# A decode block on one core: TensorE's share of the scores cut to 8 positions in every other middle step, the maximum taken behind the next products, 24 heads of W_o in two loads

## The chip, the cores and the metric

One core of a Trainium2 chip runs the whole program. The metric is device time in microseconds (us) of one execution; the time before is the median of 3 runs. Engines: TensorE (PE, with its weight loads PEld), VectorE (DVE), ScalarE (ACT), GpSimd (POOL), and SyncE (SP), which issues nearly all transfers.

## The reference

A decode step of a transformer block for a batch of 2 with one query each: layer norm, attention over a cache of 8192 positions with 32 heads of 128, output projection and residual, then a second layer norm and a gated feed-forward part with ReLU.

```python
def _A_ref(x, k_cache, v_cache, wq, wo):      # x [2,1,512], caches [2,32,8192,128]
    q = (x @ wq).reshape(B, Sq, Hq, Dh) ...
    scores = einsum("bhqd,bhkd->bhqk", q, k) * (Dh ** -0.5)
    p = softmax(scores)
    o = einsum("bhqk,bhkd->bhqd", p, v)
    return o.reshape(B, Sq, Hq * Dh) @ wo
h  = x + _A_ref(layernorm(x), ...)
h2 = h + _B_ref(layernorm(h), W_gate, W_up, W_down)   # F = 1376; down(relu(gate) * up)
```

Each cache is 134 MB in bf16, and every byte of both is needed once.

## The kernel before

**Steps.** The two batches by 16 pairs of heads make N = 32 steps; L = 31 is the last. Step i holds one pair: partitions 0 to 63 have the first head, 64 to 127 the second, and each partition has NT = 128 positions of 128 numbers, 32 KB, for K and as much for V. kbuf and vbuf have two such buffers each, used in turn. A step's K is one transfer of 4 MB and so is its V (in two or four pieces for the last three).

**Scores.** The positions of a step are shared by share(i). VectorE takes the first nv: products(i) (L335) multiplies K by the query in place, scores(i) halves the width from 128 to 8 by four additions (L350) and sums the rest (L354) into scol; then pm (L358) is the maximum of each partition. TensorE takes the last npe, in scores_pe(i): chunks of 8 positions are transposed (L309), copied to SBUF by ScalarE (L311) and multiplied by the query (L300); ScalarE copies the row (L316), TensorE turns it back (L319), and ScalarE puts it into scol (L325). npe is 24 in step 0, 16 in steps 1 to 28, 32 in steps 29 and 30, and 8 in step 31.

**Softmax.** largest(i) brings pm of all partitions together by a matmul into the PSUM tile mx_ps (L365); exponentials(i) takes the minimum nm of the negated values on VectorE (L377), and ScalarE computes the exponentials into pgz (L380) and their sums into zc.

**Values.** values(i, part) multiplies half of V by pgz in 16 matmuls (L396); after part 1 ScalarE copies the result into pv (L402). A group is four steps (the last one is cut into 2, 1 and 1). At its end diagonals picks the outputs out of pv (L411), sums adds zc over the partitions into z_ps, shares takes the reciprocal rz, and normalise writes the heads' columns ocol. Steps 30 and 31 use values_cols instead (L423), a matmul for every position.

**Output projection.** SETS lists the sets of heads of W_o, each with its first head, number of heads, partitions and place in wbig. A set has its rows spread over the partitions, so that few long runs are moved; spread(k) (VectorE) and the first lines of attend_set(k) bring ocol into the same order (or_ps), and the rest multiplies. The sets are heads 0 to 15; 16 (on 16 partitions, with a further copy, placed); 17; 18 and 19; 20 to 23; 24 to 27. Heads 28 to 31 are a load of their own. Sets are used as soon as their last group is normalised, in batch 1.

**Buffers.** mx_ps, z_ps, or_ps and the layer norm's small tiles share one PSUM buffer, the tag mx, which has one copy: each must be read before the next is written.

**Order.** The order on each engine is the program's (manual_schedule): engines run their own instructions in order and wait for one another by semaphores. SyncE's queue is in order too. The loop over steps is:

```python
for i in range(L):
    sums(i - 2); scores_pe(i); products(i)
    shares(i - 2); normalise(i - 2); attend_set(...)   # where i - 2 ends a group
    values(i - 1, 0); scores(i); largest(i); exponentials(i)
    load K(i + 2); values(i - 1, 1); diagonals(i - 1); load V(i + 1)
```

K(i+2) goes into the buffer that scores(i) has just done with, V(i+1) into that of values(i-1). Steps L-1 and L are written out behind the loop, with the loads of W_gate, W_up (into kbuf's first buffer) and W_down between, then the second layer norm and the feed-forward part (hn, g_ps L576, u_ps, d_ps L606).

Of the kernel before, what the change touches and what calls it, by code (L numbers as in the profile page):

```python
# [13 lines left out]
def _free(t, offset, dims):  # L14

    return bass.AP(tensor=t.tensor, offset=t.offset + offset, ap=[t.ap[0]] + [list(d) for d in dims])


def _dram(t, offset, dims):
    return bass.AP(tensor=t.tensor, offset=t.offset + offset, ap=[list(d) for d in dims])  # L20
# [3 lines left out]
def kernel(  # L24
# [24 lines left out]
    ROW = NT * Dh  # L49
    NG = Hq // 2  # L50
    NPE = NT // 4
    NPE_MID = NT // 8
    NPE_LAST = NT // 16
    TPC = 8
    VG = 4
    EPS = 1e-5
# [9 lines left out]

    SETS = [(0, 16, P, 0), (16, 1, 16, 16), (17, 1, P, 24), (18, 2, P, 25), (20, 4, P, 27), (24, 4, P, 32)]
    WO_T = 36  # L70
    HM = Hq - 4

    assert Sq == 1 and Hkv == Hq and Dh == P and D == KC * P and Hq == 32 and NPE % TPC == NPE_MID % TPC == NPE_LAST % TPC == 0
    assert F == 11 * P - AGAIN

    big = ctx.enter_context(tc.tile_pool(name="big", bufs=1))
# [28 lines left out]
    ocol = consts.tile([P, Hq, B], bf16)  # L105
    hm = consts.tile([P, FC, B], bf16)

    SROWS = [n * Dh // w for _, n, w, _ in SETS]
    sizes = [r for r in sorted(set(SROWS)) if r > 1]
    quot = {r: consts.tile([P, Dh // r], bf16, name=f"quot{r}") for r in sizes}  # L110
    rest = {r: consts.tile([P, r], bf16, name=f"rest{r}") for r in sizes}
    orow = [consts.tile([P, r, B], bf16, name=f"orow{k}") for k, r in enumerate(SROWS)]
    placed = consts.tile([P, B, 16], bf16)
    sel = consts.tile([B, B, HALF], bf16)

    QZ = 2 * NPE // 4
# [7 lines left out]
    N = len(steps)  # L124

    def wo_set(k):
        return wbig[:, SETS[k][3] * D:]

    def load_kv(cache, buf, i, pieces=1, which=None):
        b, g = steps[i]  # L130
# [25 lines left out]
    with tc.manual_schedule():  # L156
# [77 lines left out]
        nc.vector.tensor_copy(qz[:, :, :, QZ - 2:QZ], qT_ps.rearrange("p (g j) b -> p b g j", j=2))  # L234


        for k, ((h0, n, w, _), r) in enumerate(zip(SETS, SROWS)):
            nc.sync.dma_start(
                out=wo_set(k)[0:w, 0:r * D],
                in_=_dram(A_wo, h0 * Dh * D, ([[r * D, P]] if w == P else [[r * D, 4], [4 * r * D, 4]]) + [[1, r * D]]),  # L240
            )
        nc.sync.dma_start(
            out=wbig[:, WO_T * D:(WO_T + Hq - HM) * D].rearrange("p (h n) -> p h n", n=D),
            in_=_dram(A_wo, HM * Dh * D, [[D, P], [Dh * D, Hq - HM], [1, D]]),
# [35 lines left out]

        def share(i):

            npe = NPE_LAST if i == L else NPE if i >= L - 2 else NPE_MID if i else NPE - TPC
            return NT - npe, npe

        def scores_pe(i):


            b, g = steps[i]
            kt = kbuf[:, i % 2, :]  # L290
            nv, npe = share(i)
            U = npe // 4
            row_ps = ps.tile([2 * U, 4 * P], f32, tag="row")
            kTs = {}

            def times_q(c0):
                for k in range(0, TPC, 4):
                    u = (c0 + k) // 4
                    z0 = QZ - 2 - 2 * u
                    nc.tensor.matmul(  # L300
                        out=row_ps, lhsT=qz[:, b, g, z0:z0 + 2 * U],
                        rhs=kTs[c0][:, k * P:(k + 4) * P], start=(u == 0), stop=(u == U - 1),
                    )
# [12 lines left out]
            nc.scalar.activation(out=rows, in_=row_ps, func=ACT.Copy)  # L316
            sc_ps = ps.tile([P, 4, U, 2], f32, tag="row", name="sc_ps")
            for t in range(4):
                nc.tensor.transpose(  # L319
                    sc_ps[:, t].rearrange("p u j -> p (u j)"), rows[:, t * P:(t + 1) * P], ident_f[0:2 * U, 0:2 * U],  # L320
                )
            scols[i] = small.tile([P, NT], f32, tag="scol", name="scol")
            for j in range(2):
                r = slice(j * HALF, (j + 1) * HALF)
                nc.scalar.activation(  # L325
                    out=scols[i][r, nv:NT].rearrange("p (u t) -> p t u", t=4), in_=sc_ps[r, :, :, j], func=ACT.Copy,
                )

        def products(i):

            b, g = steps[i]
            kt = kbuf[:, i % 2, :]
            nv, _ = share(i)
            kv = _free(kt, 0, [[Dh, nv], [1, Dh]])
            nc.vector.tensor_tensor(  # L335
                out=kv, in0=kv, in1=_free(qrep, (b * NG + g) * Dh, [[0, nv], [1, Dh]]), op=ALU.mult,
            )
# [91 lines left out]

        def spread(k):  # L430

            h0, n, w, _ = SETS[k]
            if SROWS[k] == 1:
                return None
            nq = Dh // SROWS[k]
            sps = []
            for b in range(B):
                sp = small.tile([P, P], bf16, tag="spread", name="sp", bufs=4)
                nc.vector.tensor_tensor(
                    out=_free(sp, 0, [[nq, n], [1, nq]]), in0=_free(ocol, h0 * B + b, [[B, n], [0, nq]]),  # L440
                    in1=_free(quot[SROWS[k]], 0, [[0, n], [1, nq]]), op=ALU.mult,
                )
                if w != P:
                    nc.vector.tensor_copy(
                        _free(placed, b * 16, [[1, 4], [4, 4]]), _free(sp, 0, [[4, 4], [1, 4]]),
                    )
                    sp = placed[:, b, :]
                sps.append(sp)
            return sps

        def attend_set(k, sps):

            h0, _, w, _ = SETS[k]
            r = SROWS[k]
            rows = ocol[:, h0:h0 + 1, :]
            if sps is not None:
                or_ps = ps.tile([P, B, r], f32, tag="mx")
                for b in range(B):
                    nc.tensor.matmul(out=or_ps[0:w, b, :], lhsT=sps[b], rhs=rest[r], start=True, stop=True)
                rows = orow[k]  # L460
                nc.scalar.activation(out=rows[0:w], in_=or_ps[0:w].rearrange("p b c -> p c b"), func=ACT.Copy)
            for c0 in range(r):
                for c in range(KC):
                    nc.tensor.matmul(
                        out=att_ps[:, c, :],
                        lhsT=wo_set(k)[0:w, c0 * D + c * P:c0 * D + (c + 1) * P], rhs=rows[0:w, c0, :],
                        start=(k == 0 and c0 == 0 and c == 0), stop=False, skip_group_check=True,
                    )

# [8 lines left out]
        def spreads(i):  # L478

            if i not in groups or groups[i][0] < B - 1:  # L480
                return
            _, g0, n = groups[i]
            for k, (h0, m, _, _) in enumerate(SETS):
                if 2 * g0 < h0 + m <= 2 * (g0 + n):
                    yield k, spread(k)

        for i in range(L):
            if i >= 2:
                sums(i - 2)
            scores_pe(i)  # L490
            products(i)
            if i - 2 in groups:
                shares(i - 2)
                normalise(i - 2)
            for k, sps in spreads(i - 2):
                attend_set(k, sps)
            if i >= 1:
                values(i - 1, 0)
            scores(i)
            largest(i)  # L500
            exponentials(i)
            if i + 2 < N:
                load_kv(A_k_cache, kbuf, i + 2)
            if i == L - 2:
                load_kv(A_v_cache, vbuf, i, 2, [1])
            if 1 <= i < L - 1:
                values(i - 1, 1)
                diagonals(i - 1)
            if i + 1 < L:

                load_kv(A_v_cache, vbuf, i + 1, 1 if i < L - 3 else 2, [0] if i == L - 3 else None)
            if i == NG // 2:
                nc.sync.dma_start(out=wd_sb[:, FC - 1, :], in_=_dram(B_W_down, FSETS[-1][0] * D, [[D, P], [1, D]]))


        scores_pe(L)
        products(L)
        values(L - 2, 1)
        load_kv(A_v_cache, vbuf, L, pieces=4)
        for w, src, n in ((0, B_W_gate, KC), (1, B_W_up, KC // 2)):  # L520
            for c in range(0, KC, n):
                nc.sync.dma_start(  # L522
                    out=wgu[:, w, c:c + n], in_=_dram(src, c * P * F, [[F, P], [P * F, n], [1, F]]),
                )
# [123 lines left out]
```

## Time and profile before

| | |
|---|---|
| time, median of 3 runs | 662.05 us (661.96 to 662.15) |
| profiled execution | 661.76 us, span 660.0 us |
| granted TensorE clock, mean | 0.818 |
| busy: VectorE, TensorE, ScalarE | 551.9, 432.5, 154.7 us |
| moved | 281.48 MB, mean 426 GB/s |
| chain that ended last | DMA 52%, VectorE 42%, TensorE 4% |
| VectorE's idle time before products, for K | 40.1 us over 32 steps |
| VectorE's idle time before nm, for mx_ps | 23.8 us over 32 steps |

The span is the time from the first to the last instruction of the one execution that was profiled; its own time has some 1.8 us around that. In the profile's page, L335 is line 335 of the kernel. Busy digits are tenths of each of 40 equal slices of the span. In the timeline a line gives the start, the length, the engine, the source line and operation, what is written and read with the shapes, how many instructions are merged into it, and in brackets the idle time before them with what ended it. In the groups, what follows the bar is total busy time and the mean of one in ns. In the stretches of time, busy time and number of instructions of PE, PEld, DVE, ACT and POOL are followed by the granted TensorE clock, the share of DMA time and GB/s.

### The profile page before, as it was taken

The page shows a single profiled execution, that of the slowest core. Times are in us where ns is not written, and L with a number is a line of the kernel's source. Part 1 is how long each engine was busy: PE and PEld are TensorE (multiplying, and loading weights), DVE is VectorE, ACT ScalarE, POOL GpSimd, SP SyncE. Part 2 cuts the span into 40 slices and gives each one's busy share as a digit, 9 for nine tenths or more (in the row PEclk, how much of TensorE's full clock was granted, in tenths as well). Part 3 has the DMA queues.
Part 4 walks back from the last instruction along what each step waited for, and adds up shares of the span by engine and source line. Part 5 has one row for each costly group of instructions (what it writes and reads, how often), then busy time and mean ns, then how long its engine had stood idle before and what let it go on. Part 6 is the DMA issues. An engine that isn't in the chain of part 4 may idle for free.

```text
span 660.0 us, 6125 instructions
## 1 busy us (share of the span) xinstructions
PE 432.5 (66%) x2567; PEld 190.8 (29%) x2567; DVE 551.9 (84%) x327; ACT 154.7 (23%) x340; POOL 4.9 (1%) x21
## 2 busy tenths in 40 slices
PE   2725677676666557667656765676676765688676
PEld 1312222322223223222223222232222422234246
DVE  2599998888889888889988888988888998887991
ACT  1421222222122222022222212222221222222410
POOL 2000000000000000000000000000000000000000
PEclk9967987888778898877789877778987778988975
DMA  9999999999999999999999999999999999999996
GB/s 381 434 411 447 427 432 440 420 439 434 429 437 428 437 426 435 439 426 435 436 424 440 427 433 438 427 436 435 425 440 429 430 439 425 439 432 424 430 421 273
DMA packets 13331, 281.48 MB, mean 426 GB/s; under 512 B 1382, under 2 KB 2664, under 8 KB 4200
## 3 DMA queue, kind: packets, MB, share of 16 engines
q1 hardware_dynamic: 13300, 281.09, 99.1%
q8 instruction: 20, 0.33, 0.2%
q14 instruction: 7, 0.06, 0.0%
q10 hardware_dynamic: 4, 0.00, 0.0%
HBM read 281.09 MB, written 0.00 MB: 426 GB/s over the span
## 4 chain that ended last, share of the span: by engine, by line
DMA 52%; DVE 42%; PE 4%; SPq 1%; issue 1%; ACT 0%; DVEq 0%; ACTq 0%
DMA kbuf<-in_A_k_cache_dram 47%; DVE kbuf L350 20%; DVE kbuf L335 19%; DVE scol L354 3%; DMA wd_sb<-in_B_W_down_dram 3%; DMA wbig<-in_A_wq_dram 2%; PE q_ps L219 1%; PE pv_ps L396 1%; SPq L522 1%; DVE vbuf L222 0%; PE r_ps L226 0%; PE mx_ps L365 0%; PE d_ps L606 0%; ACT kT L311 0%; PE row_ps L300 0%
## 5 line engine op out<-in xcount | busy, mean ns | idle before, releaser
L396 PE MATMUL pv_ps<-vbuf,pgz 128*8 128x512 bf16 x960 | 283.5, 462 | 78.0 <-DMA vbuf<-in_A_v_cache_dram 78.0
L335 DVE TENSOR_TENSOR kbuf<-kbuf,qrep 128x14336 bf16<-128x14336 bf16 (+3 forms) x32 | 241.8, 7557 | 40.1 <-DMA kbuf<-in_A_k_cache_dram 40.1
L350 DVE TENSOR_TENSOR kbuf<-kbuf 128x1792 bf16<-128x1792 bf16 (+9 forms) x128 | 242.2, 1892 | 4.1
L396 PEld LDWEIGHTS <-pgz 128*8 128x8 bf16 x960 | 93.3, 100 | 244.1 <-issue 174.5
L380 ACT ACTIVATE pgz<-scol,nm 64x128 bf16<-64x128 f32 x64 | 25.5, 399 | 334.7 <-DVE nm L377 333.9
L311 ACT ACTIVATE kT<-t_ps 128x1024 bf16<-128x1024 bf16 x68 | 66.2, 1021 | 15.1 <-PE t_ps L309 14.6
L300 PE MATMUL row_ps<-kT,qz 128*8 128x512 bf16 (+3 forms) x136 | 42.7, 398 | 33.9 <-ACT kT L311 33.7
L365 PE MATMUL mx_ps<-nscale,pm 128*128 128x128 f32 x64 | 16.5, 343 | 65.4 <-DVE pm L358 63.2
L309 PE MATMUL t_ps<-ident,kbuf 128*128 128x128 bf16 x544 | 37.5, 222 | 0.0
L309 PEld LDWEIGHTS <-kbuf 128*128 128x128 bf16 x544 | 32.1, 100 | 11.8 <-issue 11.7
L354 DVE TENSOR_REDUCE scol<-kbuf 128x112 f32<-128x896 bf16 (+3 forms) x32 | 34.5, 1078 | 1.1
L402 ACT ACTIVATE pv<-pv_ps 8x512 f32<-8x512 f32 x30 | 17.7, 589 | 74.2 <-PE pv_ps L396 74.2
L365 PEld LDWEIGHTS mx_ps<-nscale,pm 128*128 128x128 f32 x64 | 10.5, 206 | 79.9 <-issue 49.0
L377 DVE TENSOR_REDUCE nm<-mx_ps 128x2 f32<-128x128 f32 x32 | 9.3, 291 | 23.8 <-PE mx_ps L365 23.8
L319 PE MATMUL sc_ps<-ident_f,rows 8*128 8x8 f32 (+3 forms) x128 | 14.2, 216 | 21.7 <-ACT rows L316 21.7
L300 PEld LDWEIGHTS <-qz 128*8 128x8 bf16 (+3 forms) x136 | 11.2, 84 | 51.2 <-issue 43.5
L316 ACT ACTIVATE rows<-row_ps 8x512 f32<-8x512 f32 (+3 forms) x32 | 18.8, 587 | 23.4 <-PE row_ps L300 23.4
L319 PEld LDWEIGHTS sc_ps<-ident_f,rows 8*128 8x128 f32 (+3 forms) x128 | 11.3, 149 | 39.5 <-ACT rows L316 39.5
L325 ACT ACTIVATE scol<-sc_ps 64x16 f32<-64x16 f32 (+3 forms) x64 | 12.4, 194 | 17.8 <-PE sc_ps L319 17.0
L222 DVE CAST vbuf<-q_ps 2x512 bf16<-2x512 f32 x8 | 5.4, 678 | 13.2 <-PE q_ps L219 13.2
L219 PE MATMUL q_ps<-wbig,xn 128*2 128x512 bf16 x32 | 9.2, 440 | 8.6 <-DMA wbig<-in_A_wq_dram 8.6
L358 DVE TENSOR_REDUCE pm<-scol 128x1 f32<-128x128 f32 x32 | 9.1, 285 | 3.7 <-DVE scol L354 0.5
(96 smaller groups left out, 112.4 us busy)
## 6 DMA issues: line engine op xcount, KB each, us to landing
kbuf<-in_A_k_cache_dram SPq DMA_DIRECT2D x32, 4096.0 KB, 22.1
vbuf<-in_A_v_cache_dram SPq DMA_DIRECT2D x29, 4096.0 KB, 27.3
vbuf<-in_A_v_cache_dram SPq DMA_DIRECT2D x4, 2048.0 KB, 26.1
wbig<-in_A_wq_dram SPq DMA_DIRECT2D x1, 4096.0 KB, 12.4
vbuf<-in_A_v_cache_dram SPq DMA_DIRECT2D x4, 1024.0 KB, 20.7
wbig<-in_A_wo_dram SPq DMA_DIRECT2D x1, 2048.0 KB, 22.1
wbig<-in_A_wo_dram SPq DMA_DIRECT2D x3, 512.0 KB, 22.1
kbuf<-in_B_W_gate_dram SPq DMA_DIRECT2D x1, 1376.0 KB
```

The costliest lines, as they stand in the source:

```text
L300: nc.tensor.matmul(out=row_ps, lhsT=qz[:, b, g, z0:z0 + 2 * U], rhs=kTs[c0][:, k * P:(k + 4) * P], start=(u == 0), stop=(u == U - 1),)
L309: nc.tensor.transpose(t_ps[:, k, :], kt[:, t * Dh:(t + 1) * Dh], ident)
L311: nc.scalar.activation(out=kTs[c0], in_=t_ps.rearrange("p t s -> p (t s)"), func=ACT.Copy)
L316: nc.scalar.activation(out=rows, in_=row_ps, func=ACT.Copy)
L319: nc.tensor.transpose(sc_ps[:, t].rearrange("p u j -> p (u j)"), rows[:, t * P:(t + 1) * P], ident_f[0:2 * U, 0:2 * U],)
L335: nc.vector.tensor_tensor(out=kv, in0=kv, in1=_free(qrep, (b * NG + g) * Dh, [[0, nv], [1, Dh]]), op=ALU.mult,)
L350: nc.vector.tensor_tensor(out=lo, in0=lo, in1=_free(kt, half, [[Dh, nv], [1, half]]), op=ALU.add,)
L354: nc.vector.tensor_reduce(out=scol[:, 0:nv], in_=_free(kt, 0, [[Dh, nv], [1, 8]]), axis=AXIS.X, op=ALU.add,)
L365: nc.tensor.matmul(out=mx_ps.rearrange("p a b -> p (a b)"), lhsT=_free(pms[i], 0, [[0, P]]), rhs=nscale, start=True, stop=True,)
L380: nc.scalar.activation(out=pgz[r, s, :, j, :], in_=scol[r, :].rearrange("p (u t) -> p u t", t=VG), func=ACT.Exp, scale=SCALE, bias=nm[r, j ...
L396: nc.tensor.matmul(out=pv_ps[i][r, :], lhsT=pgz[:, s, u].rearrange("p j t -> p (j t)"), rhs=vbuf[:, s, u * VG * Dh:(u + 1) * VG * Dh], sta ...
L402: nc.scalar.activation(out=pv[r, (g // 4) % 2], in_=pv_ps[i][r, :], func=ACT.Copy)
```

## The change

- share(i): npe is 8 in the odd middle steps (1 to 27) and 0 in the even ones (2 to 28), then 16, 32, 16 in steps 29, 30, 31. Step 0 keeps 24. Where npe is 0, scores_pe only names scol.
- exponentials(i-1) stands behind products(i) in step i, where it stood behind largest(i-1) in step i-1.
- values(i-1, 1) and diagonals(i-1) stand ahead of largest(i), and attend_set behind largest(i). The spread operations stay ahead of values(i-1, 0).
- W_o: the five sets after the first are two, heads 16 to 23 and 24 to 27, all on 128 partitions; the copy to placed goes.
- W_gate is loaded in four pieces, not in one.

```diff
-    NPE_MID = NT // 8
-    NPE_LAST = NT // 16
+    NPE_MID = 8
+    NPE_END = (16, 32, 16)
...
-    SETS = [(0, 16, P, 0), (16, 1, 16, 16), (17, 1, P, 24), (18, 2, P, 25), (20, 4, P, 27), (24, 4, P, 32)]
+    SETS = [(0, 16, 0), (16, 8, 16), (24, 4, 32)]
...
-            npe = NPE_LAST if i == L else NPE if i >= L - 2 else NPE_MID if i else NPE - TPC
+            npe = NPE_END[i - L + 2] if i >= L - 2 else NPE_MID * (i % 2) if i else NPE - TPC
...
             nv, npe = share(i)
+            scols[i] = small.tile([P, NT], f32, tag="scol", name="scol")
+            if not npe:
+                return
...
             scores_pe(i)
             products(i)
+            if i >= 1:
+                exponentials(i - 1)
             if i - 2 in groups:
                 shares(i - 2)
                 normalise(i - 2)
-            for k, sps in spreads(i - 2):
-                attend_set(k, sps)
+            early = list(spreads(i - 2))
             if i >= 1:
                 values(i - 1, 0)
             scores(i)
+            if 1 <= i < L - 1:
+                values(i - 1, 1)
+                diagonals(i - 1)
             largest(i)
-            exponentials(i)
+            for k, sps in early:
+                attend_set(k, sps)
             if i + 2 < N:
                 load_kv(A_k_cache, kbuf, i + 2)
...
-            if 1 <= i < L - 1:
-                values(i - 1, 1)
-                diagonals(i - 1)
...
         scores_pe(L)
         products(L)
+        exponentials(L - 1)
         values(L - 2, 1)
         load_kv(A_v_cache, vbuf, L, pieces=4)
-        for w, src, n in ((0, B_W_gate, KC), (1, B_W_up, KC // 2)):
+        for w, src, n in ((0, B_W_gate, 1), (1, B_W_up, KC // 2)):
```

More of the change, by code (lines that the diff above doesn't have):

```diff
@@ L64 @@
     AGAIN = 32
-    SETS = [(0, 16, P, 0), (16, 1, 16, 16), (17, 1, P, 24), (18, 2, P, 25), (20, 4, P, 27), (24, 4, P, 32)]
+    SETS = [(0, 16, 0), (16, 8, 16), (24, 4, 32)]
     WO_T = 36
     HM = Hq - 4
-    assert Sq == 1 and Hkv == Hq and Dh == P and D == KC * P and Hq == 32 and NPE % TPC == NPE_MID % TPC == NPE_LAST % TPC == 0
+    assert Sq == 1 and Hkv == Hq and Dh == P and D == KC * P and Hq == 32 and all(n % TPC == 0 for n in (NPE, NPE_MID, *NPE_END))
     assert F == 11 * P - AGAIN
@@ L106 @@
     hm = consts.tile([P, FC, B], bf16)
-    SROWS = [n * Dh // w for _, n, w, _ in SETS]
-    sizes = [r for r in sorted(set(SROWS)) if r > 1]
+    SROWS = [n for _, n, _ in SETS]
+    sizes = sorted(SROWS)
     quot = {r: consts.tile([P, Dh // r], bf16, name=f"quot{r}") for r in sizes}
@@ L112 @@
     orow = [consts.tile([P, r, B], bf16, name=f"orow{k}") for k, r in enumerate(SROWS)]
-    placed = consts.tile([P, B, 16], bf16)
     sel = consts.tile([B, B, HALF], bf16)
@@ L126, in wo_set @@
     def wo_set(k):
-        return wbig[:, SETS[k][3] * D:]
+        return wbig[:, SETS[k][2] * D:]
     def load_kv(cache, buf, i, pieces=1, which=None):
@@ L234 @@
         nc.vector.tensor_copy(qz[:, :, :, QZ - 2:QZ], qT_ps.rearrange("p (g j) b -> p b g j", j=2))
[L237 to L241, printed above, removed]
+        for k, (h0, n, _) in enumerate(SETS):
+            nc.sync.dma_start(out=wo_set(k)[:, 0:n * D], in_=_dram(A_wo, h0 * Dh * D, [[n * D, P], [1, n * D]]))
         nc.sync.dma_start(
@@ L321, in scores_pe @@
                 )
-            scols[i] = small.tile([P, NT], f32, tag="scol", name="scol")
             for j in range(2):
@@ L430, in spread @@
         def spread(k):
-            h0, n, w, _ = SETS[k]
-            if SROWS[k] == 1:
-                return None
+            h0, n, _ = SETS[k]
             nq = Dh // SROWS[k]
@@ L442, in spread @@
                 )
[L443 to L447, printed above, removed]
                 sps.append(sp)
@@ L451, in attend_set @@
         def attend_set(k, sps):
-            h0, _, w, _ = SETS[k]
             r = SROWS[k]
[L455 to L461, printed above, removed]
+            or_ps = ps.tile([P, B, r], f32, tag="mx")
+            for b in range(B):
+                nc.tensor.matmul(out=or_ps[:, b, :], lhsT=sps[b], rhs=rest[r], start=True, stop=True)
+            nc.scalar.activation(out=orow[k], in_=or_ps.rearrange("p b c -> p c b"), func=ACT.Copy)
             for c0 in range(r):
@@ L465, in attend_set @@
                         out=att_ps[:, c, :],
-                        lhsT=wo_set(k)[0:w, c0 * D + c * P:c0 * D + (c + 1) * P], rhs=rows[0:w, c0, :],
+                        lhsT=wo_set(k)[:, c0 * D + c * P:c0 * D + (c + 1) * P], rhs=orow[k][:, c0, :],
                         start=(k == 0 and c0 == 0 and c == 0), stop=False, skip_group_check=True,
@@ L482, in spreads @@
             _, g0, n = groups[i]
-            for k, (h0, m, _, _) in enumerate(SETS):
+            for k, (h0, m, _) in enumerate(SETS):
                 if 2 * g0 < h0 + m <= 2 * (g0 + n):
```

## The prediction, made before the change was run

> **What bounds the kernel now.** I read the page first: busy time, then the rate of the transfers in slices.
>
> ```profile
> PE 432.5 (66%) x2567; PEld 190.8 (29%) x2567; DVE 551.9 (84%) x327; ACT 154.7 (23%) x340; POOL 4.9 (1%) x21
> ...
> DMA  9999999999999999999999999999999999999996
> GB/s 381 434 411 447 427 432 440 420 439 434 429 437 428 437 426 435 439 426 435 436 424 440 427 433 438 427 436 435 425 440 429 430 439 425 439 432 424 430 421 273
> ```
>
> The DMA engines are full in all slices but the last. 281 MB at the middle's rate are some 650 us, so only the start, the end and what empties the queue can move the time. Then the timeline of two middle steps (weight loads and lines between left out):
>
> ```profile
> 312.43 0.33 SPq L133 DMA_DIRECT2D kbuf<-in_A_k_cache_dram  x1
> 312.47 0.28 DVE L358 TENSOR_REDUCE pm<-scol 128x1 f32<-128x128 f32 x1
> ...
> 312.90 0.46 PE L365 MATMUL mx_ps<-nscale,pm 128*128 128x128 f32 x2 [1.24 <-DVE pm L358]
> ...
> 313.40 0.29 DVE L377 TENSOR_REDUCE nm<-mx_ps 128x2 f32<-128x128 f32 x1 [0.64 <-PE mx_ps L365]
> ...
> 315.18 7.62 DVE L335 TENSOR_TENSOR kbuf<-kbuf,qrep 128x14336 bf16<-128x14336 bf16 x1 [1.49 <-DMA kbuf<-in_A_k_cache_dram]
> ...
> 316.94 0.33 SPq L133 DMA_DIRECT2D vbuf<-in_A_v_cache_dram  x1
> ...
> 324.89 5.00 PE L396 MATMUL pv_ps<-vbuf,pgz 128*8 128x512 bf16 x16 [3.52 <-DMA vbuf<-in_A_v_cache_dram]
> ...
> 331.76 0.33 SPq L133 DMA_DIRECT2D kbuf<-in_A_k_cache_dram  x1
> ...
> 334.55 7.63 DVE L335 TENSOR_TENSOR kbuf<-kbuf,qrep 128x14336 bf16<-128x14336 bf16 x1 [1.54 <-DMA kbuf<-in_A_k_cache_dram]
> ```
>
> VectorE waits 1.5 us for K in each step, and steps are 19.37 us apart: 8.39 MB at 433 GB/s. When K is issued (331.76) the K before it lands 2.8 us later and a V of 9.7 us stands behind that: 12.5 us of work are queued. That is how late VectorE may get before the queue runs dry.
>
> Last, the end, where compute takes over:
>
> ```profile
> 627.39 5.64 PE L396 MATMUL pv_ps<-vbuf,pgz 128*8 128x512 bf16 x16
> ...
> 641.04 0.80 PE L365 MATMUL mx_ps<-nscale,pm 128*128 128x128 f32 x2 [2.20 <-DVE rz L270]
> ...
> 650.35 1.83 PE L576 MATMUL g_ps<-hn,kbuf 128*128 128x2 bf16 x44 [0.74 <-DMA kbuf<-in_B_W_gate_dram]
> ...
> 655.57 1.56 PE L606 MATMUL d_ps<-hm,wd_sb 128*128 128x2 bf16 x44 [0.84 <-DMA wd_sb<-in_B_W_down_dram]
> ```
>
> W_down is the last data; 4.4 us of compute and store follow. The attention's own chain (mx at 641.04, hn at 650.02) is only just ahead of W_gate.
>
> **VectorE in the middle.** Prices by size:
>
> ```profile
> L335 DVE TENSOR_TENSOR kbuf<-kbuf,qrep 128x14336 bf16<-128x14336 bf16 x28 | 213.5, 7625 | 38.2 <-DMA kbuf<-in_A_k_cache_dram 38.2
> ...
> L335 DVE TENSOR_TENSOR kbuf<-kbuf,qrep 128x15360 bf16<-128x15360 bf16 x1 | 8.1, 8149 | 0.0
> ```
>
> 112 positions cost 7.63 (products), 3.89+2.02+1.09+0.63 (tree) and 1.09 (reduction): 16.34 us. 120 positions have rows too (8.15, 4.16, 2.16, 1.16, 0.66, 1.15): 17.43. On the same line 128 cost 18.53. So an odd step gains 1.09 us of work, an even one 2.19. A step without a wait for K now takes 18.06 (products at 45.76 and 63.82), of which about 1.0 is the round trip pm, mx, nm. Behind the next products the matmul has 8 us to finish, so VectorE keeps only nm's 0.2 of issue: 17.06 + 1.09 = 18.15 odd, 19.25 even, 18.70 on average. New is a wait in the seven steps that end a group: z_ps and mx_ps share one PSUM buffer, so sums(i-2) must wait for nm(i-1), and VectorE then waits for z; by the row of nm 0.64, with rz and ocol (0.20 each) 1.04, or 0.26 per step. 18.96 is 0.4 below 19.37: the K wait falls from 1.5 to a few tenths, the stream stays the clock. K is issued up to 2.5 us later in its step, so 10 us stay queued.
>
> **TensorE, ScalarE and the V loads.** The transposes, copies and small products leave: about 1060 of 6125 instructions, all hidden now, so worth nothing by themselves. The exponentials start 9 us into a step and take 1.1; the 32 value matmuls then run in one piece, by the rows 5.6 (cold) and 3.6 us (warm): done at 19.3. On the queue, V(i+1) follows K(i+2) at once instead of 4.5 us later; nothing gained, since both wait behind others. In a group's step TensorE stands from sums until nm (8.7 us); behind it are scores_pe (4.6 us to ScalarE's last copy) and, on ScalarE behind those copies, the exponentials: values end near 24, V(i+1) 5 us behind K. The maximum is then ready at 25 and asked for at 28. Cost: nothing, with 3 us in hand. The 16 heads of W_o wait for nm(25) in step 26, which has no TensorE scores to hold up.
>
> **W_o and instruction fetches.** While they are moved, three stretches of 2 us (44 to 50 us) run at 403, 372 and 416 GB/s against 432, 0.5 us lost in all; the loads of 1, 2 and 4 heads are about half of that. Head 16 alone lands in four parts, where other loads land in sixteen: 32 KB on each of four engines, 1.2 us (a 32 KB packet takes 1.21), against 0.3 if spread. In the trace's landing records the sixteen parts of the last W_down load are 4.35 us apart, and instruction packets of 16 KB (0.93 each, 20 of them) fall on single engines. A sixth fewer instructions is three packets. If these were on the slowest engines the stream ends 1.5 us sooner; if the four engines were the early ones, 0.3 later. I take -0.5, toward the rows that are seen losing. W_gate in four loads costs SyncE three issues of 0.4 us, beside 12 us of queued data: nothing.
>
> **The end.** Steps 29 to 31 have 112, 96, 112 positions on VectorE (now 96, 96, 120). K(30) lands at 607.4. Two spread operations replace eight on VectorE, 0.9 us saved, ahead of that wait for K and so lost in it. Products(30) 6.6, nm(29): 614.3. Only then may TensorE do the 8 heads of W_o (their or_ps shares mx's buffer): 0.5 + 1.1, to 615.9. scores_pe(30) as now (610.10 to 616.92) 6.8, and ScalarE's copies: 623.3. The exponentials of 29 stand behind these: 624.3. values(29,0) 3.6, mx(30) 0.5: 628.5; scores_pe(31), two chunks, 4.5: 633.0; values(29,1) 3.6: 636.7. Then pv's copy, diagonals, sums and values_cols(30), 0.65 + 4.7 as now without its wait: 642.0. So mx(31) starts 0.9 us later, up to 1.9 when scores_pe(30) begins at half clock (two chunks took 5.9 at 45.31, 4.5 at 316.84). The last V is issued at 637 to 639, while its first half, issued at 628, is on its way until 641: no loss. hn comes at 651.0 to 652.0, and g, u and hm need 4.0 without waits: d_ps can start at 655.0 to 656.0, against 655.57. With the stream's -0.5 on both: 655.0 to 655.5.
>
> **Sum.** Against the profiled execution (span 660.0, 661.76 us): middle 0, W_o and fetches -0.5, end 0 to +0.4: -0.5 to -0.1. That run is 0.3 under the median 662.05; I put the middle, -0.3, on the median: 661.8 us. No change that counts: within 0.2%, 1.3 us, about what a measurement can tell.
>
> **Rivals.** *The end runs on a slow clock* (slower). The granted clock:
>
> ```profile
> 622.00:624.00 2.00, 0.93 (x10) 0.83 (x11) 1.42 (x3) 0.90 (x4) 0.00 (x0) 1.00 0.99 426
> 624.00:626.00 2.00, 0.81 (x2) 0.08 (x1) 2.00 (x1) 1.11 (x2) 0.00 (x0) 0.67 1.01 434
> 626.00:628.00 2.00, 1.32 (x7) 0.72 (x7) 2.00 (x1) 0.94 (x3) 0.00 (x0) 0.50 0.98 418
> ```
>
> An idle 1.7 us before 622 kept 1.00, one of 2.1 us at 623 to 625 ended it, and the next 16 products took 5.64 instead of 3.62. If both halves of values(29) are cold, mx(31) slips 4 more, 4.9 in all, less what warms on the way: 4.3. With the stream's -0.5, hn 653.8 and d_ps 657.9, 2.3 behind now: 664.3. d_ps moves by a slip over 1.5 us, and the total by 1.3 from 3.3 us. For it: TensorE stands from 610.5 to 614.3, waiting for nm(29). Against: scores_pe(30) then works for 7 us. The Trainium skill (TensorE: Matmul & The Clock Gate, What's actually happening) says that an idle window of about 3.4 us halves the clock, a busy one of that length restores it, and the windows run freely. By that rule this wait starts scores_pe(30) cold and leaves values(29) warm: the slip of 1.9, and the same total. The trace agrees on the two speeds, though its drop came behind gaps of 2.1 and 1.1 us. Chance 0.20.
>
> *VectorE becomes the clock* (slower): if a step costs over 0.4 us more than I sum (a later maximum, longer group waits), it falls behind the stream; at a mean of 19.5 it is 4 us late after 28 steps, and steps 30 and 31 with it: about 665. For: even steps have 0.1 to spare. Against: sizes lie on a line. Chance 0.08.
>
> *The stream ends 1.5 us sooner and the end stays warm* (faster): 660.5. The chain that begins with K(30) moves with the stream, so it does not hold d_ps back. It needs the slowest engines to be just those that are relieved. Chance 0.08.
>
> **Numbers.** The forecast keeps 0.64: faster 0.08, same 0.64, slower 0.28. Range 660.8 to 664.8, over the first rival and most of the third.
>
> **What would show it.** K waits of VectorE near 0.3 us instead of 1.5, none on mx outside the end; the group steps' rz waiting 0.6 for z; K landings 19.35 apart; mx(31) at 641.5 to 643 and d_ps waiting for W_down by less than 0.8 or not at all. Wrong if K no longer delays the products (VectorE is the clock), if the DMA rate dips in the middle, or if mx(31) starts behind 644.

## The result: 2.2 us slower, and a new spread

The changed kernel takes 664.24 us (median of 22 runs, 661.94 to 666.34) against 662.04 (22 runs, 661.75 to 662.39): ratio 1.003, 95% interval [1.0022, 1.0038]. The forecast was 661.8. The runs before agree within 0.7 us; those of the change spread over 4.4. The profiled execution of the change took 665.48 us, span 663.7, so it stands toward the slow end; its differences below are larger than those of the medians.

The page, with the lines that answer to those of before:

```profile
PE 378.2 (57%) x2049; PEld 163.4 (25%) x2049; DVE 593.7 (89%) x319; ACT 99.5 (15%) x253; POOL 4.9 (1%) x21
...
GB/s 379 439 410 445 440 418 435 442 422 431 442 434 422 442 425 432 442 431 426 438 434 424 437 438 429 428 442 433 423 437 438 427 432 439 433 423 438 423 371 215
```

The work moved as meant: TensorE and ScalarE 54 and 55 us less, VectorE 42 more, and 1113 instructions fewer. The stream holds its rate up to slice 38. Only the last two slices, 371 and 215 GB/s, are worse than before (421 and 273). The middle, from the timeline:

```profile
304.23 0.28 DVE L375 TENSOR_REDUCE nm<-mx_ps 128x2 f32<-128x128 f32 x1
...
314.50 0.33 SPq L132 DMA_DIRECT2D kbuf<-in_A_k_cache_dram  x1
...
314.92 0.38 SPq L132 DMA_DIRECT2D vbuf<-in_A_v_cache_dram  x1
...
315.01 8.16 DVE L333 TENSOR_TENSOR kbuf<-kbuf,qrep 128x15360 bf16<-128x15360 bf16 x1 [0.21 <-DMA kbuf<-in_A_k_cache_dram]
...
334.34 8.69 DVE L333 TENSOR_TENSOR kbuf<-kbuf,qrep 128x16384 bf16<-128x16384 bf16 x1 [1.19 <-DMA kbuf<-in_A_k_cache_dram]
```

nm waits for nothing, V follows K at once, and K still ends the wait of the products, by 0.21 and 1.19 us instead of 1.5. K(30) starts the products at 606.89, half a microsecond sooner than before. So at step 30 the change is ahead. The end:

```profile
613.71 0.19 PE L447 MATMUL or_ps<-rest,sp 128*128 128x8 bf16 x2 [1.93 <-DVE nm L375]
...
615.02 1.87 PE L308 MATMUL t_ps<-ident,kbuf 128*128 128x128 bf16 x16
...
624.32 0.29 DVE L356 TENSOR_REDUCE pm<-scol 128x1 f32<-128x128 f32 x1 [2.97 <-ACT scol L323]
...
625.36 6.32 PE L394 MATMUL pv_ps<-vbuf,pgz 128*8 128x512 bf16 x16 [1.56 <-ACT pgz L378]
...
644.97 0.78 PE L363 MATMUL mx_ps<-nscale,pm 128*128 128x128 f32 x2
...
659.55 1.31 PE L596 MATMUL d_ps<-hm,wd_sb 128*128 128x2 bf16 x44
```

TensorE waits 1.93 us for nm(29), begins scores_pe(30) at 615.02, keeps VectorE waiting for its scores, and takes 6.32 us for 16 products that take 3.62 on a full clock. mx(31) comes 3.9 us later than before, d_ps 4.0. d_ps no longer waits for W_down: TensorE's chain sets the end.

### The profile page after: what moved, and what is told of

The parts are those of the page before. It is cut to its first block, busy times and chain, and to the rows that moved or that the text cites. A ratio compares the mean times of both kernels' runs of the same rounds, so it can differ in the third digit from the quotient of the medians.

```text
span 663.7 us, 5012 instructions
## 1 busy us (share of the span) xinstructions
PE 378.2 (57%) x2049; PEld 163.4 (25%) x2049; DVE 593.7 (89%) x319; ACT 99.5 (15%) x253; POOL 4.9 (1%) x21
## 4 chain that ended last, share of the span: by engine, by line
DMA 45%; DVE 45%; PE 8%; issue 1%; ACT 1%; DVEq 0%; SPq 0%; ACTq 0%
DMA kbuf<-in_A_k_cache_dram 43%; DVE kbuf L333 21%; DVE kbuf L348 19%; DVE scol L352 3%; DMA wbig<-in_A_wq_dram 2%; PE pv_ps L394 1%; PE q_ps L218 1%; PE o_ps L421 1%; PE z_ps L262 1%; DVE nm L375 1%; ACT kT L310 1%; PE row_ps L299 0%; PE t_ps L308 0%; DVE vbuf L221 0%; PE r_ps L225 0%
## 5 line engine op out<-in xcount | busy, mean ns | idle before, releaser
L394 PE MATMUL pv_ps<-vbuf,pgz 128*8 128x512 bf16 x960 | 273.4, 455 | 165.3 <-ACT pgz L378 124.3
L333 DVE TENSOR_TENSOR kbuf<-kbuf,qrep 128x15360 bf16<-128x15360 bf16 (+4 forms) x32 | 264.8, 8274 | 14.5 <-DMA kbuf<-in_A_k_cache_dram 13.5
L348 DVE TENSOR_TENSOR kbuf<-kbuf 128x1920 bf16<-128x1920 bf16 (+13 forms) x128 | 263.4, 2058 | 3.3
L352 DVE TENSOR_REDUCE scol<-kbuf 128x120 f32<-128x960 bf16 (+4 forms) x32 | 37.4, 1168 | 3.2
L310 ACT ACTIVATE kT<-t_ps 128x1024 bf16<-128x1024 bf16 x25 | 25.2, 1023 | 93.7 <-PE t_ps L308 93.7
L299 PE MATMUL row_ps<-kT,qz 128*4 128x512 bf16 (+3 forms) x50 | 20.3, 501 | 18.8 <-ACT kT L310 18.8
L308 PE MATMUL t_ps<-ident,kbuf 128*128 128x128 bf16 x200 | 20.2, 269 | 0.0
L308 PEld LDWEIGHTS <-kbuf 128*128 128x128 bf16 x200 | 17.8, 129 | 2.9 <-issue 2.6
L318 PE MATMUL sc_ps<-ident_f,rows 4*128 4x4 f32 (+3 forms) x72 | 8.6, 222 | 12.3 <-ACT rows L315 12.3
L315 ACT ACTIVATE rows<-row_ps 4x512 f32<-4x512 f32 (+3 forms) x18 | 10.6, 587 | 15.8 <-PE row_ps L299 15.8
```

Of the source, the lines that this page charges most:

```text
L299: nc.tensor.matmul(out=row_ps, lhsT=qz[:, b, g, z0:z0 + 2 * U], rhs=kTs[c0][:, k * P:(k + 4) * P], start=(u == 0), stop=(u == U - 1),)
L333: nc.vector.tensor_tensor(out=kv, in0=kv, in1=_free(qrep, (b * NG + g) * Dh, [[0, nv], [1, Dh]]), op=ALU.mult,)
L348: nc.vector.tensor_tensor(out=lo, in0=lo, in1=_free(kt, half, [[Dh, nv], [1, half]]), op=ALU.add,)
L352: nc.vector.tensor_reduce(out=scol[:, 0:nv], in_=_free(kt, 0, [[Dh, nv], [1, 8]]), axis=AXIS.X, op=ALU.add,)
L394: nc.tensor.matmul(out=pv_ps[i][r, :], lhsT=pgz[:, s, u].rearrange("p j t -> p (j t)"), rhs=vbuf[:, s, u * VG * Dh:(u + 1) * VG * Dh], sta ...
```

## Experiments

Theory: all of the loss is in the last three steps, where TensorE starts scores_pe(30) behind nm(29) and then runs at half clock. Rivals: the order alone without the clock; the new split 16, 32, 16; the middle; the stream.

**The heads of W_o ahead of the maximum again.**

```diff
-            largest(i)
             for k, sps in early:
                 attend_set(k, sps)
+            largest(i)
```

> The changed kernel with one step moved: attend_set stands ahead of largest(i) again instead of behind it, so that its or_ps no longer waits for nm, which now comes behind the next products. Theory (the end): step 29's 8 heads of W_o hold TensorE until nm(29) at 613.4 us; scores_pe(30) starts at 615.0 instead of right behind K(30) at 606.9, and the whole end of TensorE is late and on a slow clock. Then scores_pe(30) starts before 612, pm(30) no longer waits for scol (2.97 us), mx(31) starts at 640 to 642 instead of 644.97, and the time falls to 661.3 to 662.3 us, with less spread between runs than the 4.4 us of the changed kernel. Rival (the clock alone): the wait matters only through the clock, which may be as slow here since TensorE is still idle up to nm(29) for the exponentials: mx(31) above 643, time 663.5 to 664.5. Rival (the middle, or the split 16, 32, 16): no change, 664.2.

661.39 us (11 runs, 660.91 to 662.76), ratio 0.9994 [0.9985, 1.0003]: 2.85 us of the change's time are gone with one line. mx(31) starts at 642.19, a trifle later than expected, and scores_pe(30) at 613.98, not before 612: mx(29) now comes at 613.68, behind the heads, so nm(29) waits 1.03 us for it. But TensorE waits only 0.60 us in the heads and not at all behind them, and its clock is 1.00 up to 621.4, through scores_pe(30); only values(29, 0) is still slow (6.49 us).

**Fillers in the two waits.**

```diff
             largest(i)
+            if i == L - 2:
+                fill(9)      # 9 products of 128x512, read by nobody
             for k, sps in early:
...
+            if i == L - 1:
+                fill(7)
             if i >= 1:
                 values(i - 1, 0)
```

> The changed kernel with 9 products of 128x512 that nobody reads added on TensorE between largest(29) and attend_set, where it waits some 2 us for nm(29), and 7 more ahead of values(29, 0), where it waits 1.6 us for the exponentials. Nothing is taken away, so the order and every wait for data stay. Theory (the clock): these two waits drop the granted clock to a half; kept busy, scores_pe(30) takes 6.8 us instead of 8.8 and values(29, 0) 3.6 instead of 6.3, mx(31) starts at 640.5 to 642, and the time is 661 to 662.3 us. Rival (the order alone): the clock is no matter, the fillers change nothing or cost their own 1 to 3 us: 664 to 667. Rival (part): the clock still drops, since 9 products are not enough: time between.

661.09 us (660.93 to 661.43), ratio 0.9984 [0.9975, 0.9993]. The timeline of this kernel:

```profile
616.15 1.05 PE L308 MATMUL t_ps<-ident,kbuf 128*128 128x128 bf16 x16
...
624.58 3.62 PE L394 MATMUL pv_ps<-vbuf,pgz 128*8 128x512 bf16 x16
...
641.61 0.77 PE L363 MATMUL mx_ps<-nscale,pm 128*128 128x128 f32 x2
```

scores_pe(30) starts 1.1 us later than in the change, since the fillers outlast the wait, and mx(31) is still 3.4 us earlier: the same products take 3.62 us, the same 16 transposes 1.05 instead of 1.87. The granted clock is 1.00 from 608.4 to 639.1 us. Added work makes the kernel 3.15 us faster, and the spread falls from 4.4 us to 0.5. The slow clock is the loss; the order only makes the waits in which it drops.

**The old end.** Up to step 28 the change, from step 29 the order and shares of before (attend_set, values and exponentials in their old places; the exponentials of step 28 too).

```diff
-    NPE_END = (16, 32, 16)
+    NPE_END = (32, 32, 8)
...
-            if i >= 1:
+            if 1 <= i <= L - 3:
                 exponentials(i - 1)
...
```

> The changed kernel up to step 28 (8 and 0 positions on TensorE, maximum behind the next products, W_o in two loads, W_gate in four), and the order and the shares of the kernel before (32, 32, 8) in steps 29 to 31. Theory (all of the loss is in the last three steps): K(30) lands near 606.9, mx(31) starts at 640.5 to 641.5, d_ps waits for W_down again, and the time is 661.3 to 662.0 us, at or 0.5 us under the kernel before. Rival (the middle costs): VectorE is late against the stream by some us when step 29 begins, or the last loads are, and the time stays at 663.5 or more.

660.97 us (660.74 to 661.39), ratio 0.9983 [0.9974, 0.9992]. The middle costs nothing; with it the kernel is 1.1 us faster than before, more than expected. mx(31) starts at 640.70 and d_ps waits 0.85 us for W_down again.

**The two loads of W_o alone,** in the kernel before.

```diff
-    SETS = [(0, 16, P, 0), (16, 1, 16, 16), (17, 1, P, 24), (18, 2, P, 25), (20, 4, P, 27), (24, 4, P, 32)]
+    SETS = [(0, 16, P, 0), (16, 8, P, 16), (24, 4, P, 32)]
```

> The kernel before with heads 16 to 23 of W_o in one load on 128 partitions instead of four, head 16's 16-partition load and the copy to placed gone with them; nothing else. Theory (the stream's engines are evened out and small runs go): K(30) lands 0.2 to 0.5 us earlier than 607.39, and the time is 0.2 to 0.5 us under the kernel before, 661.5 to 661.8. Rival (fewer instructions made the changed kernel's stream 0.5 us earlier, not W_o): K(30) at 607.2 to 607.5 and no difference, 662.0. Rival (the four engines were the early ones): up to 0.3 us more.

662.47 us (662.26 to 662.73) against 662.08, ratio 1.0005 [0.9997, 1.0014]. Neither the theory nor its rivals: K(30) does land 0.48 us earlier (606.91), and V's first quarter of step 31 a whole microsecond (638.40 instead of 639.43), but the next quarter lands later than before (642.08, before 641.86). An instruction packet is on the transfer engines at 639.0 in this run, and from here on the parts of a load land 4.5 to 4.8 us apart instead of 3.3 (in the kernel before 3.8, and 4.4 from 637 us on). The evening-out is real, and it is taken back beside one packet; that this packet met an engine that was already last fits the landings, but the trace doesn't name the engines. The 0.39 us themselves are not clear of the noise, since the interval includes 1.

**The middle alone,** old W_o, old W_gate, old end.

> The kernel before with only the middle of the change: 8 and 0 positions on TensorE in steps 1 to 28 and the maximum behind the next products there. W_o in six sets and a load, W_gate in one load and the last three steps are those of the kernel before. Theory (the middle's gain comes with fewer instructions to fetch, the two loads of W_o cost 0.4): 660.4 to 660.8 us, under the 660.97 of the kernel with the old end, and W_down's first load lands at 654.2 to 654.6. Rival (the two loads cost only beside the old middle): 661.0. Rival (the gain needs the new W_o or W_gate): 661.5 to 662.1.

661.33 us (661.08 to 661.73), ratio 0.9988 [0.9979, 0.9997]. The middle brings 0.8 us without any change to the weights' loads. W_down's first load lands at 654.87 (655.53 before), behind the 654.2 to 654.6 expected. Here the two loads of W_o, which the kernel with the old end has besides, are worth 0.36 us by the medians, where in the old middle they cost 0.39: the expectation had the wrong sign. The intervals of the two kernels overlap, though (0.9983 and 0.9988 of the kernel before, 0.0009 either way), so 0.36 isn't clear of the noise.

**The instructions put back,** in the kernel with the old end.

```diff
                 values(i - 1, 1)
                 diagonals(i - 1)
+                idle(18)      # 18 products of 8x2 numbers, read by nobody
```

> The kernel with the old end (steps 29 to 31 as before, the rest of the change in place) plus 18 products of 8x2 numbers that nobody reads on TensorE behind the values of each of the 28 middle steps: 1008 instructions (with their weight loads), which brings the number back to that of the kernel before, for about 1 us of idle TensorE time in a step. Theory (instruction packets of 16 KB take 0.93 us of one transfer engine each, and the slowest engine sets the landings): 20 packets instead of 16, W_down's first load at 655.2 to 656.0 instead of 654.70, and 661.5 to 662.5 us instead of 660.97. Rival (the gain is from something else in the middle, such as the earlier V loads): 16 or 20 packets, but 660.8 to 661.2 us.

662.41 us (662.04 to 662.64), 1.44 above the kernel with the old end. The page's queues, first of that kernel, then with the instructions put back:

```profile
q8 instruction: 16, 0.26, 0.1%
```

```profile
q8 instruction: 20, 0.33, 0.2%
```

Four packets more, W_down's first load 1.17 us later (655.87 against 654.70), and the whole gain of the middle is gone. The landing records say where: from 600 to 638.6 us every load lands within 0.2 us of the same load in the kernel with the old end, its sixteen parts 3.2 to 3.4 us apart. A packet is on the transfer engines at 638.1, and from the load that lands at 642.15 on the parts are 4.4 to 4.5 us apart. So the delay comes in one step beside one packet, the seventeenth, and not bit by bit from four. In the two other profiles with 20 packets the first load that lands after the seventeenth spreads too: from 3.8 to 4.4 us in the kernel before (packet at 630.9), from 3.3 to 4.5 with the two loads of W_o alone (639.0). In the kernel with the old end, with 16, the parts stay 3.3 us apart to the last load.

The experiment isn't clean, though. The added products take TensorE 0.6 us in each step, and in this run the attention's chain is later as well:

```profile
602.32 6.46 PE L394 MATMUL pv_ps<-vbuf,pgz 128*8 128x512 bf16 x16
...
608.71 0.49 PE L363 MATMUL mx_ps<-nscale,pm 128*128 128x128 f32 x2
...
655.91 1.51 PE L612 MATMUL d_ps<-hm,wd_sb 128*128 128x2 bf16 x44
```

values(28, 0) meets a slow clock for longer (6.46 us, with the old end alone 5.30), mx(29) comes at 608.71 instead of 605.99, mx(31) at 643.05 instead of 640.70, and d_ps no longer waits for W_down: both are there at 655.9. W_down alone would have held d_ps back as long, but how much of the 1.44 us is the packet's and how much TensorE's is not separated.

**The old split in the changed order.**

```diff
-    NPE_END = (16, 32, 16)
+    NPE_END = (32, 32, 8)
```

> The changed kernel with one size changed: TensorE's share in steps 29, 30, 31 is 32, 32, 8 as before, not 16, 32, 16; all of the order is the changed kernel's. Theory (the order at the end costs, not the split): scores_pe(29) gets longer behind its wait for nm(28), exponentials(28) and values(28) about 2.5 us later, scores_pe(30) still waits for nm(29); step 31 has one chunk less on TensorE, so the end is about as late: 663 to 665 us, with a spread of some us. Rival (the split is the cost, since scores_pe(31) with two chunks stands ahead of values(29, 1)): 661.0 to 662.3.

661.56 us (660.92 to 663.45), in two clusters: six runs up to 661.56, five from 662.72. The profiled one is the slowest: mx(29) is late at 615.09, since scores_pe(29) is longer, and mx(31) comes at 644.67. Here TensorE is at full clock for scores_pe(30) and slow for values(29, 0) (6.50 us). The median speaks for the rival, the slow cluster for the theory. What made the fast cluster fast was not profiled; the split is part of the chain, not its cause by itself.

**No TensorE scores in the middle.** The old end with NPE_MID = 0.

> The kernel with the old end, with no TensorE scores at all in steps 1 to 28: all 128 positions on VectorE. By the sum in the prediction a step costs VectorE 19.25 us, 19.5 with a group's waits, against 19.37 of the stream, and some 450 instructions fewer are fetched. Theory (VectorE is just at the bound): it falls 2 to 4 us behind by step 29 and never waits for K in the second half; the queued 10 us hide this from the stream, but the last steps start late: 661.5 to 664 us. Rival (steps are cheaper than summed and the stream still leads, with two packets of instructions fewer): 660.5 to 661.0. Rival (a step costs over 19.8): above 668.

661.07 us (660.70 to 661.88). Its products, one step apart:

```profile
529.59 8.68 DVE L333 TENSOR_TENSOR kbuf<-kbuf,qrep 128x16384 bf16<-128x16384 bf16 x1
...
548.70 8.69 DVE L333 TENSOR_TENSOR kbuf<-kbuf,qrep 128x16384 bf16<-128x16384 bf16 x1
```

No wait for K here, and 0.8 us in the whole run: 19.11 us is VectorE's own step with 128 positions, where the prediction had 19.25. It is not late in step 29, as the theory had it: its products start at 588.75 there, 1.7 us before those of the kernel with the old end (590.48), which has the same order in the last steps. (In the changed kernel they start at 587.57.) Two packets fewer (14) bring nothing more.

**The change twice more.**

> The changed kernel once more, one look. Its runs lie between 661.94 and 666.34 us. Theory (the clock's phase decides): the time goes with the granted clock while scores_pe(30) and values(29) run; in an execution near 662 scores_pe(30) takes about 7 us and the first half of values(29) near 4, mx(31) starts at 641.5 to 642.5; near 665 they take about 9 and 6, mx(31) at 644 to 645. Rival (the stream varies): the landings of V in the last steps differ between executions by as much as the times do.

> As the look before, a further execution of the changed kernel, to have more than one time: each microsecond of time should be found again in the lengths of scores_pe(30) and values(29) (theory), or in the landings of V (rival).

661.85 and 664.37 us: one at the fast end of the spread, one at the median. Stretches of the first, then of the second (granted clock third from the right):

```profile
612.00:614.00 2.00, 0.61 (x5) 0.37 (x5) 2.00 (x3) 0.73 (x2) 0.00 (x0) 1.00 1.02 442
614.00:616.00 2.00, 1.85 (x48) 1.76 (x48) 2.00 (x1) 0.45 (x2) 0.00 (x0) 1.00 1.06 459
```

```profile
612.00:614.00 2.00, 0.20 (x2) 0.13 (x2) 2.00 (x3) 0.14 (x1) 0.00 (x0) 0.91 1.02 442
614.00:616.00 2.00, 1.90 (x43) 1.90 (x43) 2.00 (x1) 0.05 (x1) 0.00 (x0) 0.50 0.99 426
...
620.00:622.00 2.00, 1.36 (x11) 0.84 (x11) 1.17 (x2) 1.26 (x2) 0.00 (x0) 0.88 0.92 393
622.00:624.00 2.00, 1.01 (x6) 0.41 (x5) 0.00 (x0) 0.85 (x3) 0.00 (x0) 0.97 0.99 426
```

and their timelines, again in this order:

```profile
613.63 0.19 PE L447 MATMUL or_ps<-rest,sp 128*128 128x8 bf16 x2 [1.22 <-DVE nm L375]
...
614.89 1.05 PE L308 MATMUL t_ps<-ident,kbuf 128*128 128x128 bf16 x16
...
623.31 5.30 PE L394 MATMUL pv_ps<-vbuf,pgz 128*8 128x512 bf16 x16 [1.56 <-ACT pgz L378]
...
641.91 0.77 PE L363 MATMUL mx_ps<-nscale,pm 128*128 128x128 f32 x2
```

```profile
613.63 0.20 PE L447 MATMUL or_ps<-rest,sp 128*128 128x8 bf16 x2 [1.93 <-DVE nm L375]
...
614.96 1.87 PE L308 MATMUL t_ps<-ident,kbuf 128*128 128x128 bf16 x16
...
625.25 6.30 PE L394 MATMUL pv_ps<-vbuf,pgz 128*8 128x512 bf16 x16 [1.56 <-ACT pgz L378]
...
644.84 0.77 PE L363 MATMUL mx_ps<-nscale,pm 128*128 128x128 f32 x2
```

or_ps starts at the same time in both. From the first transposes to the values it takes 8.42 and 10.29 us, the values 5.30 and 6.30: 2.9 of the 2.93 us between the two mx(31). By the landing records of the trace the last V of step 30 is there at 635.91 and 636.11: the stream is not it. The wait ahead of or_ps was 1.22 us in the one and 1.93 in the other, since values(28) ended 0.7 us earlier in the second.

The windows also tell when the clock changed. If it is either 1.00 or 0.50, then 0.91 between 612 and 614 means 0.36 us at half, so it fell at 613.64; in the same way it rose at 620.48 and fell again at 623.88. The steps are 6.84 and 3.40 us long. The profiled execution of the change gives 613.80, 620.64 and 624.04: 6.84 and 3.40. The first of the two rose at 607.24 and fell at 624.32: 17.08, five times 3.42. So the clock changes only on a grid of about 3.41 us, which lies elsewhere in each execution. The clock records in the traces of all 14 runs bear this out: every change lies within 0.002 us of a grid of 3.413 us, and no value but 1.00 and 0.50 occurs. What TensorE does within one cell of the grid then seems to decide. In the cell that ended in the fall at 613.64, TensorE had 1.06 us of value products and 0.4 of small ones. In the execution of 661.85 us the cell from 610.66 to 614.07 had 1.35 us of value products, and the clock held.

**W_gate in one load,** in the kernel with the old end.

> The kernel with the old end and, besides, W_gate in one load as before. Theory (the four loads cost only SyncE's issue time, under queued data): 660.8 to 661.1 us, no difference from 660.97. Rival (four loads are a part of the gain or of the loss): more than 0.2 us either way.

661.04 us (660.93 to 661.48) against 660.97: no difference, as the prediction had it.

**The exponentials of 29 ahead of scores_pe(30).**

```diff
-            scores_pe(i)
+            if i < L - 1:
+                scores_pe(i)
             products(i)
             if i >= 1:
                 exponentials(i - 1)
+            if i == L - 1:
+                scores_pe(i)
```

> The changed kernel with one swap in step 30 alone: products(30) and exponentials(29) stand ahead of scores_pe(30), so that ScalarE does the exponentials of 29 right behind nm(29), at about 613.7 us, and not behind scores_pe(30)'s copies. TensorE still waits for nm(29) in attend_set. Theory (two delays in a row on ScalarE and TensorE, each cooling the clock): values(29, 0) follows scores_pe(30) without the gap of 1.6 us; on a full clock it takes 3.6 us instead of 6.3, mx(31) starts at 641 to 642.5, and the time is 661 to 662.3 with a small spread. Rival (the first wait alone cools it): scores_pe(30) still 8.8 us, but 1.5 us are gained by the order: 662.3 to 663.3, with a spread of 1 to 2 us.

660.87 us (ten runs from 660.72 to 661.10, one at 662.52), ratio 0.9984 [0.9975, 0.9993]: the lowest median of all, and with one swap the change beats both kernels. From its timeline:

```profile
622.81 3.62 PE L394 MATMUL pv_ps<-vbuf,pgz 128*8 128x512 bf16 x16
...
640.73 0.79 PE L363 MATMUL mx_ps<-nscale,pm 128*128 128x128 f32 x2 [0.86 <-DVE rz L266]
```

values(29, 0) follows on a full clock, though scores_pe(30) began at half. The windows of this kernel:

```profile
614.00:616.00 2.00, 1.73 (x44) 1.71 (x43) 2.00 (x1) 1.17 (x5) 0.00 (x0) 0.82 1.02 442
616.00:618.00 2.00, 1.74 (x10) 0.74 (x8) 1.97 (x2) 1.94 (x2) 0.00 (x0) 0.50 0.83 360
618.00:620.00 2.00, 2.00 (x19) 1.34 (x19) 1.93 (x3) 0.96 (x1) 0.00 (x0) 0.83 1.13 475
```

It fell at 615.28 and rose at 618.68, one cell of 3.40 us. It fell although the wait for nm(29) was only 0.71 us here, where 1.22 us had held: the length of the wait does not decide. The cell before had 0.84 us of value products, and 1.6 us of small products that did not save it. That wide products (128x512) count and small ones hardly fits these falls (0.90 us of value products in the cell before the fall at 613.80, 1.01 before that at 624.32). It doesn't fit all cells: in the execution of 661.85 us the clock held behind the cell from 614.07 to 617.48, with 0.59 us of wide products and 2.1 of small ones, mostly transposes; in that of 664.37 us it fell behind the cell from 620.47 to 623.88, with 1.19 us of wide ones. Of the 1317 cells at full clock in all traces, the clock held behind each of the 770 with 1.4 us or more of wide products and fell behind each of the 252 with less than 0.5; between, it did both. What exactly counts stays open. The cell at the slow clock does not matter here: mx(31) waits for VectorE again.

## Why the prediction was wrong

**The middle was right.** VectorE's wait for K fell from 40.1 to 13.5 us in total and did not vanish; rz waits 0.69 us for z in step 29 (0.64 summed); the stream kept its pace. That VectorE would be just under the stream is borne out by the kernel without TensorE scores, which waits 0.8 us for K in all and loses nothing yet.

**The stream's -0.5 was right at step 30 and did not hold to the end.** I credited it to W_o and gave the instructions a small part. At step 30 that is what the runs show: K(30) lands 0.48 us sooner with the two loads of W_o alone, and 0.07 sooner (607.32) with the middle alone. At W_down's first load it is the other way round: 0.50 us later with the two loads alone (656.03 against 655.53), 0.66 sooner with the middle alone. What the prediction had not weighed is that a single instruction packet late in the run may undo an evened load. The instructions, which I had called worth nothing but for three packets, may be the larger term: putting 1008 back cost 1.44 us, though not by packets alone for certain. Middle and loads together make the kernel with the old end 1.1 us faster, where I had 0.5.

**The end is the step that failed.** I took scores_pe(30) at 6.8 us and values(29, 0) at 3.6, as on a full clock, with "up to 1.9" of slip for a cold start, of which 1.0 was for the clock. On the clock that was granted the transposes to the last copy took 9.3 us instead of 7.4, and the values 6.32: 4.6 us more. 0.9 of it was made up by K(30), and so nm(29) and the heads of W_o, coming sooner, and some 0.7 in scores_pe(31) and behind it. mx(31) was to start at 641.5 to 642.5 with the stream's gain; it starts at 644.97, and at 641.91 in the execution of 661.85 us. The forecast describes the fast end of what the changed kernel does. The first rival, "the end runs on a slow clock", priced at 664.3, meets its median, 664.24, and has the right mechanism, but the closeness is partly luck: its 4 us were two cold halves of values(29), where scores_pe(30) lost 1.9, the first half 2.7, and the second half ran warm in 3.62; and from mx(31) to d_ps it takes 13.6 us in the execution of 664.37, where the kernel with the fillers needs 12.9 without its wait for W_down. I gave it 0.20 because TensorE works for 7 us after the wait; but it was at half clock for 6.84 us, nearly all of them, and the clock fell once more 3.40 us later, ahead of the values.

The prediction weighed a rule of the Trainium skill (TensorE: Matmul & The Clock Gate, What's actually happening): windows of about 3.4 us that run freely, and an idle one halves the clock. The grid of 3.40 to 3.42 us agrees. That a window must be idle does not: here the clock fell with 1.5 us of work in the window, with 2.4 in the last experiment, and in the profiled execution behind a window that 128x2 products filled throughout (641.10 to 644.52). The prediction's own use of it, scores_pe(30) cold and values(29) warm, came out in none of the three executions: scores_pe(30) and values(29, 0) were cold at 664.37 and 665.48 us, and only values(29, 0) at 661.85. Its reading of the trace before was also off: the drop, at 624.69, lies inside the gap of 2.1 us and not behind a second one.

**Two smaller terms.** "The last V: no loss" was wrong in the profiled execution: its last quarters are issued at 638.2 and 640.0, when the transfer engines that were ahead had run dry (233 GB/s from 638 to 640). It did not count, since d_ps came later still. And TensorE stood for 0.98 us inside values_cols(31), waiting for nothing the profile shows, in the profiled run as in that of 661.85 us:

```profile
652.86 0.93 PE L421 MATMUL o_ps<-pgz,vbuf 128*128 128x2 bf16 x29 [0.98 <-issue]
```

In the execution of 664.37 us it stood for 0.61. An instruction packet is on the transfer engines at 650.6 in the profiled run; that TensorE waited for it is possible and was not tested, and in the run with the old split a packet at 647.3, at the first half of the same products, brings no such wait. The stall is part of why the profiled run is slower than that of 664.37 us, whose mx(31) is only 0.13 us earlier.

## What to carry to other kernels

Where a chain at the end of a kernel has one to two microseconds in hand, count its waits before its work: moving a step behind another engine's long operation adds an idle stretch, and the clock behind that stretch can cost more than the stretch itself; a few unread products in the wait are a cheap cover. In a kernel whose stream is the bound, work that is hidden may still have a price, because its instructions are fetched through the same transfer engines; here 1008 of them cost up to 1.44 us, not all of it shown to be theirs. A wide spread between runs of one program is a reading, not noise: two profiles, a fast one and a slow one, named the place.

## What the runs showed that I had not expected

- The clock of TensorE changes on a grid of about 3.41 us whose place differs between executions; where it lies against one short wait is worth 2.9 us of the end.
- Sixteen useless products made the changed kernel 3.15 us faster (664.24 to 661.09) and its spread 0.5 us instead of 4.4.
- 1008 instructions that do nothing went with 1.44 us. They are four packets of 16 KB, 0.07 MB of 281, each 0.88 to 1.04 us long; in all three profiles with 20 packets the parts of a load spread by 0.5 to 1.2 us more beside the seventeenth. Part of the 1.44 us may be TensorE's, whose chain was late in that run too.
- A better-balanced load early on brought K(30) 0.48 us sooner and W_down 0.50 later. That the later packet fell on an engine that was already behind is the likely reading, and not shown.
